# A planner that lets PV and transposes go ahead of MoE matmuls only when they can begin as early

## The chip, the cores and the metric

The kernel runs on one core of a Trainium2 chip. The metric is the time of one execution on the device, in microseconds (us). The time of a kernel is the median of three runs; beside it stands one execution taken by the hardware profiler. The core has five engines that run their own instruction queues: TensorE (PE; its weight loads are shown as PEld), VectorE (DVE), ScalarE (ACT), GpSimd (POOL) and SyncE (SP). Here POOL and SP issue the DMAs.

## What is computed

Sliding-window attention with a distance bias over 8 batches, 8 heads, 576 positions and 64 columns a head, followed by a dense layer pair with an activation on all 4608 tokens:

```python
scores = scale * np.matmul(q, k.transpose(0, 1, 3, 2))
mask = (rel >= 0) & (rel < 128)                       # rel = query position - key position
scores = np.where(mask, scores + bias[None], -1000000000.0)
attn = np.exp(scores - np.max(scores, axis=-1, keepdims=True))
attn = attn / (np.sum(attn, axis=-1, keepdims=True) + 1e-09)
x = np.matmul(attn, v)                                # then (4608, 512): heads side by side
h = x @ w_in                                          # 512 -> 2048
g = h * np.cos(h)
out = g @ w_out                                       # 2048 -> 512
```

## The kernel before

**Attention.** The work is cut into 64 units: for each batch, five blocks of 128 queries (the last of 64), the three middle blocks in two halves of four heads. Units go in pairs. For a unit TensorE makes the scores (`scores`, L556), ScalarE takes the exponential (`exps`, L583), VectorE multiplies by a table of the bias and the window (`mask`, L602), and TensorE multiplies by V with a column of ones that gives the sums (`pv`; L618 and L622 for edge blocks, L630 and L632 for middle blocks; 16 matmuls of 65 columns for a unit pair's middle blocks). VectorE divides (`norm`, L667 and L669). The result must be transposed to serve as the moving operand of the first product: on TensorE (`x_pe`, L709 and L690, and a copy to SBUF) for units that are needed soon, by a transposing DMA on SP's queue (`x_dma`) for the others.

**MoE.** Tokens go in nine chunks of 512. The first product of a chunk (`moe1`, L747; chunk 0 in smaller blocks, `moe1_block`, L772) takes 64 matmuls of 512 columns into 16 banks' worth of results; each bank gets a sine with a shifted phase on ScalarE (L752) and a multiplication on VectorE (L756) that writes `gT`. The second product (`moe2`, L800) is 64 matmuls a chunk, 16 for each 128 tokens; a copy (L807 on ScalarE or L808 on VectorE) and a store on SP follow.

**Order in the program.** For chunk c the program names the first product, then some eight units of attention that later chunks need (`QUOTA`), then the second product. The PSUM tensor `ps` has 8 banks: 0 and 1 for the second product, 2 and 3 for PV, 4 to 7 for scores; the first product of a chunk uses 2 to 7. So the first product of the next chunk comes after this chunk's attention in these banks, while the second product, in its own, can be put anywhere between.

**The planner.** The order of the instructions on each engine is not the program's: `Plan.schedule` lists the operations by a simulated clock. Each operation has an occupancy (`occ`) and a latency (`lat`) in ns, a priority (`pri`: 0 transposes, 1 PV, 2 scores, 5 first product, 6 second product) and, on TensorE, a mode (0 for MoE, PV and most transposes, 1 for scores, 2 for the transposes of q and k of the first two batches). `reach` says when an operation's inputs are there: 53 ns after the end of what another engine made, where TensorE waits. A candidate's start `st` is the later of that and of the time the engine is free; on TensorE 110 ns (`SWITCH`) are added for a change of mode, and 40 ns if the inputs come after the engine is free. `pick_pe` chooses among the candidates: `soon` is the earliest start of all; an operation with a priority under 5 that can start within an allowance of `soon` goes first, by priority; otherwise the candidate with the best priority among those that start at `soon`. Since TensorE works through its queue in the listed order, an operation that is chosen before its inputs are there holds up what is behind it.

The end of a DMA is reckoned by one of several formulas, by engine and kind; in this kernel operations with a DMA are given to "sp" and "pool" only.

Of the kernel before, what the change touches and what calls it, by code (L numbers as in the profile page):

```python
# [34 lines left out]
class Plan:  # L35
# [58 lines left out]
    def schedule(self, filler=None, fill=(0, 0)):  # L94
# [4 lines left out]
        mode, table = 0, 0  # L99
# [4 lines left out]
        def reach(o, e):  # L104
            t = 0
            for d, data in o.preds.items():
                if data == ORDER or self.held(d, data, e):
                    t = max(t, d.start + d.occ)
                elif d.dma is None and d.eng[0] == e:
                    t = max(t, d.end + 28)  # L110
                else:
                    t = max(t, d.end + (53 if e == "pe" else 36))
            return t

        def pick_pe(cand):
            soon = min(st for st, _ in cand)
            first = [(st, o) for st, o in cand if o.pri < 5 and st <= soon + 160]
            if first:
                return min(first, key=lambda c: (c[1].pri, c[1].seq))
            near = [(st, o) for st, o in cand if st <= soon]  # L120
            return min(near, key=lambda c: (c[1].pri, c[1].seq))
# [5 lines left out]
        while avail:  # L127
            phase = next((t for t in tables if left[t]), None)
            best = None
            for e in ENG:  # L130
                cand = []
                for o in avail:
                    if e not in o.eng or (o.table is not None and o.table != phase):
                        continue
                    at = reach(o, e)
                    st = max(free[e], at)
                    if e == "pe":
                        if o.mode != mode:
                            st += self.SWITCH
                        if at > free[e]:  # L140
                            st += 40
                    cand.append((st, o))
                if not cand:
                    continue
                if e == "pe":
                    st, o = pick_pe(cand)
                else:
                    soon = min(st for st, _ in cand)
                    st, o = min(((st, o) for st, o in cand if st <= soon + 40),
                                key=lambda c: (c[1].pri, c[1].seq))  # L150
                key = (st, o.pri, o.seq)
                if best is None or key < best[0]:
                    best = (key, e, o)
            (st, _, _), e, o = best
            avail.remove(o)
            if o.table is not None and o.table != table:
                st += self.TABLE
            if len(o.eng) > 1:
                o.fn, o.occ, o.lat = o.fn[e], o.occ[e], o.lat[e]
                o.eng = (e,)  # L160
            if e == "pe":
                while filler and mode == 0 and free[e] + self.FILL + 30 < st and (
                        fill[0] <= free[e] < fill[1]):
                    p = self.op("pe", filler, r=["zeros"], occ=self.FILL, lat=self.FILL + 100)
                    self.all.pop()
                    p.start, p.end = free[e], free[e] + self.FILL
                    free[e] += self.FILL
                    order.append(p)
                if st < self.COLD:
                    o.lat += o.occ  # L170
                    o.occ *= 2
            o.start = st
            free[e] = st + o.occ
            if o.dma is not None:
                if e == "sp" and o.dma[0] in "tx":
                    cross = max(cross, st + self.CROSS, min(wire + self.BACK, st + 6000)) + o.lat
                    o.end = max(cross, st + o.occ + 1400) + 500
                elif e == "sp" and o.dma[0] == "s":
                    o.end = st + o.occ + 1800 + o.lat
                elif e == "sp":  # L180
                    first = max(first, st + 1400) + o.lat
                    wire = max(wire, min(first, 5600))
                    o.end = max(first, st + o.occ + 1400) + 500
                else:
                    wire = max(wire, st + 2300) + o.lat
                    o.end = max(wire, st + o.occ + 1400) + 500
            else:
                o.end = st + o.lat
            if e == "pe":
                mode = o.mode  # L190
            if o.table is not None:
                table = o.table
                left[o.table] -= 1
            order.append(o)
            for s in o.succs:
                s.npred -= 1
                if s.npred == 0:
                    avail.append(s)
# [752 lines left out]
```

## Time and profile before

| | before |
|---|---|
| median of 3 runs | 314.29 us (313.84 to 314.87) |
| profiled execution | 314.18 us |
| its span | 312.4 us |
| TensorE matmul busy | 303.3 us, 2678 instructions |
| VectorE, ScalarE, POOL busy | 192.3, 202.4, 97.6 us |
| second product L800, first product L747 | 131.6 and 111.6 us busy |
| scores L556 | 20.7 us busy |
| PV L618, L622, L630, L632 | 8.2, 4.9, 15.0, 15.0 us busy |

Busy times of TensorE overlap where matmuls are in flight together. A row of the groups names the line, the engine, the operation, output and inputs, the shape, the count, then busy us and mean ns of one, then the engine's idle time just ahead of them and what ended most of it. A row of the timeline gives the start, the duration, the instruction, a count and, in brackets, the idle time before it. A row of the waits gives who waited for whom, then total us, number of times, and the longest. A few per cent of the matmul records are missing from the trace; the weight loads of L747 and L800 are complete (512 and 592).

### The profile page before, as it was taken

What the parts mean: (1) busy time and instruction counts of PE and PEld (TensorE: products, weight loads), DVE (VectorE), ACT (ScalarE), POOL (GpSimd) and SP (SyncE); (2) the same over time, 40 slices, a digit from 0 to 9 for tenths busy, and PEclk for the clock granted to TensorE, in tenths of its full rate; (3) what the DMA queues carried; (4) which work ended last, traced back from release to release, by engine and by line L of the source; (5) the groups of instructions that cost most, each with busy time, mean ns of one, the idle gap of its engine ahead of it and who ended that gap; (6) DMA issues with size and microseconds to landing.
All of it is one profiled execution on the core that took longest, in us unless ns stands there. A gap on an engine that the chain in (4) does not pass through costs nothing.

```text
span 312.4 us, 6647 instructions
## 1 busy us (share of the span) xinstructions
PE 303.3 (97%) x2678; PEld 160.5 (51%) x2721; DVE 192.3 (62%) x405; ACT 202.4 (65%) x270; POOL 97.6 (31%) x123
## 2 busy tenths in 40 slices
PE   7899999999999999999999999999999999999996
PEld 4689755445544454445444544455445544444444
DVE  6588667584848576748586758576766886353000
ACT  5697865885767677777677558754874868362211
POOL 8998340049132731382054605280000000000000
PEclk9999999999999999999999999999999999999999
DMA  8999999999979995999599999999641320001112
GB/s 108 163 203 207 207 168 192 177 130 179 150 118 179 96 181 111 176 110 154 94 118 149 160 117 138 155 151 131 128 109 44 78 67 2 34 0 68 69 67 101
DMA packets 150334, 38.97 MB, mean 125 GB/s; under 512 B 138912, under 2 KB 145312, under 8 KB 150304
## 3 DMA queue, kind: packets, MB, share of 16 engines
q0 software_dynamic: 100960, 18.23, 76.2%
q1 hardware_dynamic: 49344, 20.33, 31.3%
q8 instruction: 21, 0.34, 0.5%
q14 instruction: 9, 0.07, 0.1%
HBM read 36.70 MB, written 9.44 MB: 148 GB/s over the span
## 4 chain that ended last, share of the span: by engine, by line
PE 90%; DMA 3%; POOL 3%; issue 1%; DVE 1%; ACT 1%; POOLq 0%; ACTq 0%
PE ps L800 39%; PE ps L747 34%; PE ps L556 5%; PE ps L772 5%; DMA w_inb<-in_moe_w_in_dram 3%; PE ps L630 2%; PE ps L632 2%; PE ps L618 2%; POOL vp L384 1%; PE ps L497 1%; DVE gT L756 1%; POOL krows L376 1%; PE ps L622 1%; PE ps L709 1%; POOL qrows L376 0%
## 5 line engine op out<-in xcount | busy, mean ns | idle before, releaser
L800 PE MATMUL ps<-w_outb,gT 128*128 128x512 bf16 (+2 forms) x561 | 131.6, 373 | 2.3 <-issue 1.3
L747 PE MATMUL ps<-xT,w_inb 128*128 128x512 bf16 x502 | 111.6, 379 | 0.5
L756 DVE TENSOR_TENSOR gT<-ps,cos 128x512 bf16<-128x512 f32 x128 | 85.7, 689 | 40.5 <-ACT cos L752 29.8
L752 ACT ACTIVATE cos<-ps,halfpi 128x512 f32<-128x512 f32 x128 | 85.2, 687 | 22.1 <-PE ps L747 16.6
L583 ACT ACTIVATE p<-ps 128x1024 bf16<-128x1024 f32 x64 | 62.1, 1021 | 33.3 <-PE ps L556 33.2
L800 PEld LDWEIGHTS ps<-w_outb,gT 128*128 128x128 bf16 x592 | 52.8, 98 | 55.3 <-DMA w_outb<-in_moe_w_out_dram 0.2
L747 PEld LDWEIGHTS ps<-xT,w_inb 128*128 128x128 bf16 x512 | 49.8, 98 | 60.1 <-issue 0.8
L394 POOL DMA_DIRECT2D qnat<-in_q_dram x30 | 25.3, 877 | 71.3 <-DMA qt<-qnat 71.3
L602 DVE TENSOR_TENSOR p<-p,emask 128x1024 bf16<-128x1024 bf16 x59 | 39.6, 682 | 9.5 <-ACT p L583 9.3
L807 ACT ACTIVATE ob<-ps 128x512 f32<-128x512 f32 (+2 forms) x23 | 13.3, 579 | 41.7 <-PE ps L800 41.5
L384 POOL DMA_DIRECT2D vp<-in_v_dram x40 | 34.0, 896 | 9.1 <-PE ps L622 5.0
L394 POOL DMA_DIRECT2D knat<-in_k_dram x30 | 25.3, 880 | 30.7 <-DMA kt<-knat 28.3
L556 PE MATMUL ps<-qt,kt 64*128 64x128 bf16 (+1 forms) x576 | 20.7, 213 | 0.3 <-DVE qt L513 0.3
L556 PEld LDWEIGHTS ps<-qt,kt 64*128 64x128 bf16 x576 | 14.7, 95 | 11.1 <-ACT p L583 6.3
L669 DVE TENSOR_TENSOR xnat<-ps,rec 128x256 bf16<-128x256 f32 x48 | 18.3, 420 | 0.4
L808 DVE COPY ob<-ps 128x512 f32<-128x512 f32 x14 | 9.6, 687 | 13.5 <-PE ps L800 13.5
L630 PEld LDWEIGHTS ps<-vp,p 128*128 128x128 bf16 x192 | 12.7, 97 | 8.5 <-issue 8.4
L772 PE MATMUL ps<-xT,w_inb 128*128 128x128 bf16 x256 | 16.4, 219 | 0.4 <-DMA w_inb<-in_moe_w_in_dram 0.4
L630 PE MATMUL ps<-vp,p 128*128 128x65 bf16 x192 | 15.0, 193 | 0.3
L772 PEld LDWEIGHTS ps<-xT,w_inb 128*128 128x128 bf16 x256 | 14.5, 98 | 1.1 <-DMA w_inb<-in_moe_w_in_dram 0.5
L632 PE MATMUL ps<-vp,p 128*128 128x65 bf16 x192 | 15.0, 193 | 0.0
L782 DVE TENSOR_TENSOR gT<-ps,cos 128x512 bf16<-128x512 f32 x16 | 10.7, 689 | 3.2 <-ACT cos L779 2.9
(63 smaller groups left out, 159.4 us busy)
## 6 DMA issues: line engine op xcount, KB each, us to landing
out_dram<-ob SPq DMA_DIRECT2D x35, 256.0 KB, 3.6
vp<-in_v_dram POOLq DMA_DIRECT2D x32, 128.0 KB, 6.4
qnat<-in_q_dram POOLq DMA_DIRECT2D x24, 128.0 KB, 5.9
knat<-in_k_dram POOLq DMA_DIRECT2D x24, 128.0 KB, 4.8
w_outb<-in_moe_w_out_dram POOLq DMA_DIRECT2D x4, 512.0 KB, 21.7
w_inb<-in_moe_w_in_dram POOLq DMA_DIRECT2D x3, 512.0 KB, 12.1
qrows<-in_q_dram POOLq DMA_DIRECT2D x1, 576.0 KB, 15.4
krows<-in_k_dram POOLq DMA_DIRECT2D x1, 576.0 KB, 17.4
```

The lines of the kernel that those rows point to most:

```text
L384: op("pool", [lambda e, t=t, rows=rows: e.dma_start(vp[b % 2][0:rows, t, :, 0:64], v[b, :, 128 * t:128 * t + rows, :].rearrange("h p d -> ...
L394: fns.append(lambda e, t=t, rows=rows: e.dma_start(nat[which][0:rows, t, :, :], src[b, :, 128 * t:128 * t + rows, :].rearrange("h p d -> p ...
L556: ins = e.matmul(ps[:, banks[x], c0:c0 + n_], keys_ap(b, x, pr, kc), query_ap(b, x, pr, qb, n_), start=not acc, stop=stop)
L583: op("act", lambda e: e.activation(P[i][:, 0:1024], ps[:, banks[0]:banks[0] + 2, :].rearrange("p a b -> p (a b)"), ACTF.Exp, scale=0.125), ...
L602: op("dve", lambda e: e.tensor_tensor(p, p, m, ALU.mult), r=[("P", i), ("EM", 0), ("EM", 1)], w=[("P", i)], occ=600, lat=690, pri=1)
L630: e.matmul(o, P[i][:, c0:c0 + 128], V[:, qb - 1, h, 0:65], start=True, stop=False)
L632: ins = e.matmul(o, P[i][:, c0 + 128:c0 + 256], V[:, qb, h, 0:65], start=False, stop=True)
L747: op("pe", lambda e, kc=kc: e.matmul(ps[:, bank, :], w_in[:, kc, 128 * fc:128 * fc + 128], xT[:, kc, r0:r0 + CH], start=(kc == 0), stop=(k ...
L752: op("act", lambda e: e.activation(cosb[ci][:, :], ps[:, bank, :], ACTF.Sin, bias=halfpi[:, 0:1]), r=["halfpi"], w=[("B", bank), ("cos", c ...
L756: op("dve", lambda e: e.tensor_tensor(gT[gi][:, fc, :], ps[:, bank, :], cosb[ci][:, :], ALU.mult), r=[("cos", ci)], w=[("B", bank)] + [("g ...
L772: ins = e.matmul(ps[:, bank, 128 * i:128 * i + 128], w_in[:, kc, 128 * fc:128 * fc + 128], xT[:, kc, t0:t0 + 128], start=(kc == 0), stop=( ...
L800: op("pe", lambda e, t=t, fc=fc, bank=bank, j0=j0, j1=j1: e.matmul(ps[:, bank, 0:j1 - j0], gT[gi][:, fc, 128 * t:128 * t + 128], w_out[:, ...
```

## The change

Two edits in `schedule`. In `pick_pe` the allowance of 160 ns is kept for operations whose mode differs from that of TensorE's last operation; for those of the same mode it is 0. So after a MoE matmul, a PV or a transpose (mode 0), another PV or transpose is preferred over a MoE matmul only if it can start at `soon`; scores (mode 1) are still preferred up to 160 ns after it. In the reckoning of DMA ends, the branch for plain loads on "sp" now also holds for "act".

```diff
             soon = min(st for st, _ in cand)
-            first = [(st, o) for st, o in cand if o.pri < 5 and st <= soon + 160]
+            first = [(st, o) for st, o in cand if o.pri < 5 and
+                     st <= soon + (160 if o.mode != mode else 0)]
             if first:
                 return min(first, key=lambda c: (c[1].pri, c[1].seq))
...
                 elif e == "sp" and o.dma[0] == "s":
                     o.end = st + o.occ + 1800 + o.lat
-                elif e == "sp":
+                elif e == "sp" or e == "act":
                     first = max(first, st + 1400) + o.lat
```

## The prediction

> **What bounds the kernel now.** I read the page first, then the groups of instructions by line, then the waits of the weight-load unit, and then the timeline around single PV steps.
>
> ```profile
> span 312.4 us, 6647 instructions
> ...
> PE 303.3 (97%) x2678; PEld 160.5 (51%) x2721; DVE 192.3 (62%) x405; ACT 202.4 (65%) x270; POOL 97.6 (31%) x123
> ...
> PEclk9999999999999999999999999999999999999999
> ```
>
> TensorE is busy for 97% of the span, at full clock in every slice. So the time is TensorE's work plus what it loses between its instructions. Busy time alone cannot show that loss, because one matmul's tail lies over the next one's start. The groups with shapes apart give the MoE product's duration, the groups of TensorE the idle time ahead of PV, the timeline the pace:
>
> ```profile
> L800 PE MATMUL ps<-w_outb,gT 128*128 128x512 bf16 x529 | 128.1, 379 | 2.3 <-issue 1.3
> ```
>
> ```profile
> L630 PE MATMUL ps<-vp,p 128*128 128x65 bf16 x192 | 15.0, 193 | 0.3
> L618 PE MATMUL ps<-vp,p 128*128 128x65 bf16 x128 | 8.2, 193 | 0.7 <-ACT p L583 0.5
> ```
>
> ```profile
> 102.80 1.89 PE L800 MATMUL ps<-w_outb,gT 128*128 128x512 bf16 x8
> ```
>
> One MoE matmul is shown as 379 ns, but eight in a row take 1.89 us: (1890 - 379) / 7 = 216 ns from start to start. A matmul that starts up to 379 - 216 = 163 ns late therefore leaves no idle time in the matmul rows, and PV's idle of 0.3 and 0.7 us is only the rest. I count lost time from start to start, over 216 ns. The weight loads show it more openly:
>
> ```profile
> PEld ps L630 <- issue: 8.4, 22, 0.5
> ...
> PEld ps L618 <- issue: 3.7, 11, 0.6
> ...
> PEld ps L709 <- DVE xnat L669: 1.8, 7, 0.4
> ```
>
> These are the first loads of PV (L630 for the middle blocks, L618 for the edge blocks) and of the transposes of normalised tiles (L709). Part of each wait is harmless. Compare a PV that was late with one that was not:
>
> ```profile
> 182.27 0.69 DVE L602 TENSOR_TENSOR p<-p,emask 128x1024 bf16<-128x1024 bf16 x1
> 182.70 0.38 PE L800 MATMUL ps<-w_outb,gT 128*128 128x512 bf16 x1
> 183.07 0.10 PEld L630 LDWEIGHTS ps<-vp,p 128*128 128x128 bf16 x1 [0.48 <-issue]
> 183.10 0.19 PE L630 MATMUL ps<-vp,p 128*128 128x65 bf16 x1
> ```
>
> ```profile
> 41.88 0.59 PE L800 MATMUL ps<-w_outb,gT 128*128 128x512 bf16 x2
> 42.10 0.10 PEld L618 LDWEIGHTS ps<-vp,p 128*128 128x128 bf16 x1
> 42.31 0.19 PE L618 MATMUL ps<-vp,p 128*128 128x65 bf16 x1
> ```
>
> In the second, the load is made 0.21 us ahead, under the MoE matmul before it, and PV follows without a loss. In the first, the multiplication by the mask ends at 182.27 + 0.69 = 182.96, PV starts 0.14 us after that, and it is 183.10 - 182.70 = 0.40 us behind the MoE matmul: 0.40 - 0.216 = 0.18 us are lost. Its load had idled 0.48 us, so an idle time up to 0.48 - 0.18 = 0.30 us costs nothing, and all above it is TensorE time lost. MoE matmuls that were ready stood behind PV in the queue for that long.
>
> **The change part by part.**
>
> The second edit (what a DMA from ACT is reckoned at) costs nothing: every operation with a DMA in this kernel is given to SP or to POOL, so the added case never occurs.
>
> The first edit acts where TensorE's last operation has mode 0 (MoE, PV, transposes) and a PV or a transpose could begin up to 160 ns after the MoE matmul that could begin at once. The old rule took PV there; the new one takes the MoE matmul and looks again 216 ns later. No instruction is added or removed. Which PVs are these? The planner adds 40 ns when data come late, so the allowance covers data up to 120 ns late. It counts 53 ns from VectorE's end to TensorE's start, where the rows above show 140: about 90 more. So a PV that the old rule took early should lose between 0.09 and 0.21 us on the chip, and one that the planner held ready less than 0.09. In idle time of its load that is 0.39 to 0.51 against under 0.39. Thirteen of the PV loads behind a MoE matmul have 0.43 to 0.51, and none has more. The first, the largest and the last of the thirteen:
>
> ```profile
> 47.27 0.10 PEld L630 LDWEIGHTS ps<-vp,p 128*128 128x128 bf16 x1 [0.43 <-issue]
> ...
> 242.83 0.10 PEld L630 LDWEIGHTS ps<-vp,p 128*128 128x128 bf16 x1 [0.51 <-issue]
> ...
> 248.74 0.10 PEld L630 LDWEIGHTS ps<-vp,p 128*128 128x128 bf16 x1 [0.43 <-issue]
> ```
>
> That the largest stops where the allowance ends is why I take these waits for the planner's choice. The thirteen idle 6.1 us in all; less 13 x 0.30 = 3.9 this is 2.2 us lost, about 0.17 each. Behind one more MoE matmul such a PV has its data 216 - 120 = 96 ns ahead or more by the planner's clock. The chip needs 90 of these, so the whole wait goes, not only the planned part: **-2.2 us**.
>
> The Trainium skill, TensorE: Matmul & The Clock Gate, section Back-to-back issue gap, gives about 131 ns per matmul of 512 columns as the sustained rate. By that one MoE matmul would not cover waits above 131 ns, and an estimated 0.5 us of the 2.2 would stay. The trace disagrees, with its 216 ns.
>
> The transposes have the same edit but less to give, because the chip starts them sooner than the planner thinks:
>
> ```profile
> 116.90 0.81 PE L800 MATMUL ps<-w_outb,gT 128*128 128x512 bf16 x3
> ...
> 117.58 0.11 PEld L709 LDWEIGHTS ps<-ident,xnat 128*128 128x128 bf16 x2 [0.36 <-DVE xnat L669]
> 117.58 0.28 PE L709 MATMUL ps<-ident,xnat 128*128 128x128 bf16 x2
> ```
>
> The last of the three MoE matmuls starts at 116.90 + 0.81 - 0.38 = 117.33, so the transpose loses 117.58 - 117.33 - 0.216 = 0.03 us. Three of the seven waits are of this kind: **-0.1 us**.
>
> What comes back: deferred steps shift TensorE's grid, and other PVs meet it at new places. A PV held ready by less than 90 ns still stalls. If PVs fall evenly over the 216 ns between two starts, 90/216 of them wait, 45 ns on the mean, 19 over all; for the 22 + 11 = 33 waits of L630 and L618 that is 0.6 us, against about 0.3 that the waits shorter than the thirteen hold now. **+0.3 us**; the bounds are -0.3 (all go) and 33 x 45 ns - 0.3 = +1.2 (each meets the mean).
>
> The deferred PV itself delays what waits for it, by 216 - 170 = some 50 ns on the mean: the normalisation on VectorE, the transposes (over SP's queue for most units), the banks for the next pair's PV, POOL's loads of V into the buffer that a batch has left, and the next chunk's first product. The cover is the second product (L800), which TensorE has in reserve. Up to the starts of chunks 1, 2, 3 and 4 so many of its loads were made (the second x):
>
> ```profile
> 0.00:55.10 55.10, 14.12 (x55) 5.08 (x60) 1.00 1.47 178
> 0.00:88.70 88.70, 29.66 (x118) 11.10 (x128) 1.00 1.56 172
> 0.00:120.20 120.20, 42.80 (x170) 15.89 (x184) 1.00 1.54 162
> 0.00:151.90 151.90, 56.48 (x226) 20.96 (x242) 1.00 1.50 157
> ```
>
> Of 64 a chunk, 4, 0, 8 and 14 were left. The tight one is the second:
>
> ```profile
> 87.23 1.42 PEld L800 LDWEIGHTS ps<-w_outb,gT 128*128 128x128 bf16 x8
> 88.77 0.31 PEld L747 LDWEIGHTS ps<-xT,w_inb 128*128 128x128 bf16 x2
> ```
>
> ```profile
> 87.68 0.76 DVE L669 TENSOR_TENSOR xnat<-ps,rec 128x256 bf16<-128x256 f32 x2
> ```
>
> Eight matmuls of 216 ns follow the last PV of that chunk; the normalisation that frees its banks ends at 87.68 + 0.76 = 88.44, 0.33 us before the next chunk's load. So one matmul may be taken from behind this PV at no cost, a second for 0.1: **+0.1**, between 0 and 0.2.
>
> Where PV and scores are both near, scores keep the allowance and can now go first:
>
> ```profile
> 109.10 0.19 PE L622 MATMUL ps<-vp,p 128*128 128x65 bf16 x1
> 109.23 0.62 PE L556 MATMUL ps<-qt,kt 64*128 64x128 bf16 x16
> ```
>
> Scores start 0.13 us behind PV's last matmul, where PV's own matmuls follow each other at 30 ns: 0.10 for the change of mode. Swapping the two does not change the number of such changes: 0. A pair that is torn apart would pay 0.1, and I take the same for the way back.
>
> In the first 20 us there is little MoE work to put in front, and steps of attention may change places among themselves. The trace shows no such order. TensorE has 20 - 16.57 = 3.4 us idle there, and one step moved is a scores group, 0.6 us by the row above:
>
> ```profile
> 0.00:20.00 20.00, 16.57 (x244) 11.72 (x247) 12.97 (x48) 14.18 (x18) 18.86 (x30) 1.00 1.23 151
> ```
>
> I take 0, since with that much idle time TensorE mostly waits for loads there, and keep -0.5 and +0.6 for the range.
>
> Sum: -2.2 - 0.1 + 0.3 + 0.1 = -1.9 us. The profiled execution took 314.18 us (1.8 around its span), so 312.3; the median of the runs is 314.29, 0.1 above it, so **312.4 us**. Ends: -2.2 - 0.1 - 0.3 - 0.5 = -3.1 gives 311.2, and -2.3 + 1.2 + 0.2 + 0.6 = -0.3 gives 314.0.
>
> **The rivals.** A measurement of this kernel can tell about 0.3%, 0.94 us, from no change.
>
> Only what the matmul rows show as idle can be won: 0.3 + 0.7 = 1.0 us, 313.3. For it: the rest lies under a running matmul's tail. Against: 216 ns from start to start holds wherever nothing waits, so a late start moves all that follows. The Trainium skill, Perfetto Trace Analysis, calls matmul busy time a bad metric at its opening, because matmuls are pipelined. Chance 0.08, 0.05 of it beyond 0.94 us.
>
> Nothing moves: the planner held these PVs ready, the masks came late on the chip, and the new rule picks as the old one did. 314.3. For it: the planner's times are reckoned, and the chip's may lag by as much. Against: a lag has no reason to stop at 0.51, where the allowance ends. Chance 0.09.
>
> Slower: the reserve of the second product runs out in chunks 0 to 2 before the next chunk's first matmul may start. From PV's last load (just ahead of 87.23) to the banks' release pass 88.44 - 87.23 = 1.2 us, all of it idle if no reserve is left by then: 3 x 1.2 = 3.6, less the 1.9 won, +1.7 and 316.0. It decides once more matmuls are drawn ahead than the 4, 1 and 8 that are to spare, by some 13 more over the three (2.8 us, the 1.9 and the 0.94). For it: chunk 1 ends at exactly 128, and every wait removed draws a matmul ahead. Against: of the thirteen only 1, 1 and 3 lie in these chunks. Chance 0.11.
>
> **How the numbers follow.** The forecast has 0.68. That the first 20 us alone decide has 0.04, half of it faster and a quarter each for the others. Faster by over 0.3%: 0.68 + 0.05 + 0.02 = 0.75. Within 0.3%: 0.03 + 0.09 + 0.01 = 0.13. Slower: 0.11 + 0.01 = 0.12. The range is 311.2 to 314.8: the forecast's own ends are 311.2 and 314.0, and 314.8 takes in the rival in which nothing moves with half of the 0.94 above it; the slower one is left out.
>
> **What would show it.** Right: at most four PV loads behind a MoE matmul idle over 0.40 us; the waits of L630 and L618 fall together from 12.1 us towards 10; the instruction counts stay; the gain grows by some 0.1 to 0.5 us a chunk up to 251 us, and stays to the end. Wrong: the same thirteen idle times (nothing moved); new waits of L747 for VectorE at the starts of chunks 1 to 3 (the reserve is gone); or waits of 0.31 to 0.39 at most PVs (the 90 ns came back).

## The result and the profile after

| | before | changed |
|---|---|---|
| median (22 runs each) | 314.92 us (313.84 to 316.75) | 313.44 us (312.26 to 316.94) |
| ratio | | 0.9958, 95% interval 0.9939 to 0.9977 |
| profiled execution, span | 314.18, 312.4 us | 314.44, 312.5 us |

The change makes the kernel faster by 0.42%, 1.3 us (0.7 to 1.9). The profiled execution of the changed kernel is one of its longer ones: its span shows no gain at all. That is the first thing to read from its page, where DMAs and SP's queue stand in the chain that ended last, which they did not to this extent before:

```profile
span 312.5 us, 6695 instructions
...
PE 304.3 (97%) x2722; PEld 160.9 (51%) x2722; DVE 191.2 (61%) x401; ACT 204.9 (66%) x274; POOL 97.6 (31%) x123
...
PE 83%; DMA 7%; SPq 4%; POOL 3%; ACT 1%; issue 1%; DVE 0%; POOLq 0%; ACTq 0%
```

The waits of the weight loads (who waited for whom, total us, times, longest) have the gain and what took it back:

```profile
PEld ps L631 <- issue: 6.0, 20, 0.5
...
PEld ps L619 <- issue: 2.8, 10, 0.5
...
PEld ps L748 <- issue: 1.9, 3, 1.4
PEld ps L557 <- DMA kt<-knat: 1.6, 2, 1.2
...
PEld ps L619 <- DMA vp<-in_v_dram: 0.7, 1, 0.7
PEld ps L631 <- DMA vp<-in_v_dram: 0.7, 2, 0.4
...
PEld ps L748 <- DVE xnat L670: 0.4, 2, 0.2
```

(All lines are one higher than before.) PV's own waits went from 8.4 + 3.7 to 6.0 + 2.8 and the 1.4 that are put down to V, and the transposes' row is gone. Two long waits are new: 1.37 us of the first product (L748) at the start of chunk 6 and 1.16 us of the scores (L557) in chunk 5. On the timeline:

```profile
200.98 0.14 PEld L557 LDWEIGHTS ps<-qt,kt 64*128 64x128 bf16 x6 [1.16 <-DMA kt<-knat]
...
217.94 0.13 PEld L748 LDWEIGHTS ps<-xT,w_inb 128*128 128x128 bf16 x2 [1.37 <-issue]
217.97 0.38 PE L748 MATMUL ps<-xT,w_inb 128*128 128x512 bf16 x1 [0.90 <-DMA xT<-xfirst]
```

The second product still had matmuls to give at that place (369 of 384 loads made), but they are listed behind the first product's. From start to start the wait of the scores cost 0.83 us and that of the first product 1.07: 1.9 us in this execution.

The PV of 108.65, which before was 0.20 us late, shows the change itself. Before:

```profile
105.43 3.19 PE L800 MATMUL ps<-w_outb,gT 128*128 128x512 bf16 x14 [0.16 <-issue]
108.62 0.10 PEld L618 LDWEIGHTS ps<-vp,p 128*128 128x128 bf16 x1 [0.50 <-issue]
```

It now stands behind one more MoE matmul. The last of the three starts at 107.89 + 0.81 - 0.38 = 108.32, and PV follows at 0.22 us, its load idle for a harmless 0.28:

```profile
107.89 0.81 PE L801 MATMUL ps<-w_outb,gT 128*128 128x512 bf16 x3
...
108.48 0.10 PEld L619 LDWEIGHTS ps<-vp,p 128*128 128x128 bf16 x1 [0.28 <-issue]
108.54 0.19 PE L619 MATMUL ps<-vp,p 128*128 128x65 bf16 x1
```

A kernel's time has three parts that the profiles keep apart: the first 36 us, the stretch from the first to the last load of the second product, and a tail of 2.7 us. The middle one, called the stretch below, is read from one row of a kernel, the first and last start of the loads. Before and changed:

```profile
L800 PEld LDWEIGHTS ps<-w_outb,gT x592: 95/98/99, 35.7 to 309.7; 128*128 128x128 bf16 x198
```

```profile
L801 PEld LDWEIGHTS ps<-w_outb,gT x592: 95/98/99, 36.1 to 309.8; 128*128 128x128 bf16 x198
```

That is 274.0 and 273.7 us: 0.3 less, with 1.9 us of late DMAs in it.

### The profile page after: what moved, and what is told of

Same layout as the page of the kernel before. It is cut to its first block, busy times and chain, and to the rows that moved or that the text cites. A ratio compares the mean times of both kernels' runs of the same rounds, so it can differ in the third digit from the quotient of the medians.

```text
span 312.5 us, 6695 instructions
## 1 busy us (share of the span) xinstructions
PE 304.3 (97%) x2722; PEld 160.9 (51%) x2722; DVE 191.2 (61%) x401; ACT 204.9 (66%) x274; POOL 97.6 (31%) x123
## 4 chain that ended last, share of the span: by engine, by line
PE 83%; DMA 7%; SPq 4%; POOL 3%; ACT 1%; issue 1%; DVE 0%; POOLq 0%; ACTq 0%
PE ps L801 37%; PE ps L748 31%; PE ps L557 5%; PE ps L773 4%; DMA w_inb<-in_moe_w_in_dram 3%; DMA xT<-xfirst 3%; SPq L404 2%; DMA kt<-knat 2%; SPq L735 2%; PE ps L631 1%; PE ps L633 1%; PE ps L619 1%; POOL vp L385 1%; PE ps L498 1%; POOL krows L377 1%
## 5 line engine op out<-in xcount | busy, mean ns | idle before, releaser
L801 PE MATMUL ps<-w_outb,gT 128*128 128x512 bf16 (+2 forms) x592 | 136.5, 374 | 0.0
L748 PE MATMUL ps<-xT,w_inb 128*128 128x512 bf16 x512 | 112.3, 379 | 0.9 <-DMA xT<-xfirst 0.9
L757 DVE TENSOR_TENSOR gT<-ps,cos 128x512 bf16<-128x512 f32 x128 | 86.1, 689 | 41.3 <-ACT cos L753 30.3
L748 PEld LDWEIGHTS ps<-xT,w_inb 128*128 128x128 bf16 x512 | 49.8, 98 | 61.2 <-issue 1.9
L808 ACT ACTIVATE ob<-ps 128x512 f32<-128x512 f32 (+2 forms) x25 | 14.5, 581 | 41.3 <-PE ps L801 41.2
L557 PE MATMUL ps<-qt,kt 64*128 64x128 bf16 (+1 forms) x576 | 20.5, 211 | 1.2 <-DMA kt<-knat 0.7
L557 PEld LDWEIGHTS ps<-qt,kt 64*128 64x128 bf16 x576 | 14.6, 94 | 11.7 <-ACT p L584 5.9
L631 PEld LDWEIGHTS ps<-vp,p 128*128 128x128 bf16 x192 | 12.9, 97 | 6.8 <-issue 6.0
L631 PE MATMUL ps<-vp,p 128*128 128x65 bf16 x192 | 15.1, 193 | 0.4 <-DMA vp<-in_v_dram 0.2
L809 DVE COPY ob<-ps 128x512 f32<-128x512 f32 x12 | 8.2, 680 | 9.8 <-PE ps L801 9.8
L633 PEld LDWEIGHTS ps<-vp,p 128*128 128x128 bf16 x192 | 12.5, 97 | 0.1
```

The source lines that it names most:

```text
L557: ins = e.matmul(ps[:, banks[x], c0:c0 + n_], keys_ap(b, x, pr, kc), query_ap(b, x, pr, qb, n_), start=not acc, stop=stop)
L631: e.matmul(o, P[i][:, c0:c0 + 128], V[:, qb - 1, h, 0:65], start=True, stop=False)
L633: ins = e.matmul(o, P[i][:, c0 + 128:c0 + 256], V[:, qb, h, 0:65], start=False, stop=True)
L748: op("pe", lambda e, kc=kc: e.matmul(ps[:, bank, :], w_in[:, kc, 128 * fc:128 * fc + 128], xT[:, kc, r0:r0 + CH], start=(kc == 0), stop=(k ...
L757: op("dve", lambda e: e.tensor_tensor(gT[gi][:, fc, :], ps[:, bank, :], cosb[ci][:, :], ALU.mult), r=[("cos", ci)], w=[("B", bank)] + [("g ...
L801: op("pe", lambda e, t=t, fc=fc, bank=bank, j0=j0, j1=j1: e.matmul(ps[:, bank, 0:j1 - j0], gT[gi][:, fc, 128 * t:128 * t + 128], w_out[:, ...
```

## The experiments

The theory to start with (A): the change wins 2 us of PV stalls, and the late DMAs are its own doing. In chunks 4 and 5 the new plan puts the transposing DMAs of q ahead of two x transposes on SP's queue (180.91 in place of 184.49, 213.71 in place of 216.84), where they run beside POOL's loads of V. The rival (B): such waits come and go from run to run.

**SP's order undone, and SP's order alone.** In the changed kernel the q transposes of chunks 4 and 5 are put back; in the kernel before they are brought forward. All other queues keep their order.

```diff
+        sp = [o for o in self.order if o.eng[0] == "sp"]
+        for q in [o for o in sp if o.dma in ("trq0", "trq1")][4:6]:
+            i = sp.index(q)
+            q.start = [o for o in sp[i:] if o.dma[0] == "x"][1].start + 1      # undone
+            # alone: [o for o in sp[:i] if o.dma[0] == "x"][-2].start - 1
+        self.order.sort(key=lambda o: (o.start, rank[id(o)]))
```

> The changed kernel with one thing undone: in chunks 4 and 5 the transposing DMAs of q go back behind the two x transposes that stood ahead of them before the change; every other queue keeps the order of the changed kernel. Theory A (the change won about 2 us of PV stalls, and part of it was given back because it pulled the q transposes ahead of two x transposes on SP's queue, so that they run into POOL's loads of V): the 1.07 us wait of the first product at the start of chunk 6 and the 0.83 us wait of the scores in chunk 5 shrink below 0.3 us each, the x transposes of chunk 5 land within 0.5 us of 216.5, and the ratio to the kernel before is 0.990 to 0.994 (311.8 to 313.0 us). Rival B (such waits for DMAs come and go from run to run, whatever the order): waits of 0.5 us or more appear here as well, and the ratio stays at 0.996.

> The kernel before with one thing of the change alone: in chunks 4 and 5 the transposing DMAs of q are put ahead of the two x transposes, as the change did; TensorE's order is that of before. Theory A (the order on SP's queue costs): the last x transposes of chunk 5 that chunk 6 needs land at 217.5 to 218.5 in place of 216.8, TensorE waits there, and the time is 0.5 to 1.5 us over the kernel before (ratio 1.002 to 1.005). Rival B (run to run): same time, ratio 0.998 to 1.002, the waits of PV unchanged.

Undone: 314.23 us, ratio 0.9984 (0.9965 to 1.0003), no better than the change as it is; by the times alone no gain over the kernel before is clear here. Alone: 314.44 us, ratio 1.0003 (0.9984 to 1.0023). Late DMAs appear in both, at other places: at the start of chunk 5 in the first, and of chunk 3 in the second, whose SP queue is that of the kernel before up to there.

```profile
185.48 0.11 PEld L753 LDWEIGHTS ps<-xT,w_inb 128*128 128x128 bf16 x2 [0.87 <-DMA xT<-xnat]
```

```profile
122.84 0.11 PEld L752 LDWEIGHTS ps<-xT,w_inb 128*128 128x128 bf16 x2 [1.32 <-DMA xT<-xnat]
```

So the part of theory A on SP's order falls: undoing it wins nothing, and the wait turns up with TensorE's old order too.

**The rule for PV alone.**

```diff
-                     st <= soon + (160 if o.mode != mode else 0)]
+                     st <= soon + (0 if o.mode == mode and o.pri == 1 else 160)]
```

> The new rule for PV alone; transposes and the first matmuls with the bias keep the allowance of 160 ns. Theory A (the gain is in PV; the transposes lose only 0.03 us each, and the first 40 us are 0.3 us later in the changed kernel because steps of the start changed places there): stalls of PV as in the changed kernel (0.6 us in all after 20 us), the first load of the second product at 35.7 us as before and not at 36.1, SP's order as in the changed kernel, so ratio 0.993 to 0.997. Rival C (the transposes carry the gain, or the whole start is needed): ratio 0.998 to 1.000.

313.25 us, ratio 0.996 (0.9942 to 0.9978), the same as the whole change. The gain is PV's. The first load of the second product came at 37.0 us here and not at the 35.7 expected, though TensorE's order at the start is that of before: the first 36 us vary from run to run by more than the 0.3 us that I had wanted to explain.

**A larger allowance.** 320 ns in place of 0.

> The allowance for operations of the same mode is 320 ns in place of 0 (160 before). Theory A (a PV taken before its data holds up ready MoE matmuls, and all that time is lost to TensorE): nearly every PV and transpose is taken early, some 45 of them by 55 to 340 ns by the planner's clock, 10.7 us in all, and the chip adds up to 90 ns to each PV; so 9 to 14 us over the kernel before, 324 to 329 us. Rival D (TensorE's rest hides under matmul tails or is made up later, because something else paces the chunks): under 4 us slower, 319 us at most.

324.70 us, ratio 1.0313 (1.028 to 1.0345): 9.8 us slower, in the range of theory A. The waits of the same three rows grow to

```profile
PEld ps L631 <- issue: 10.6, 21, 0.7
PEld ps L619 <- issue: 6.3, 13, 1.0
...
PEld ps L710 <- DVE xnat L670: 4.4, 12, 0.6
```

from 8.4, 3.7 and 1.8, by 7.4 us in all, and the stretch grows by 8.9:

```profile
L801 PEld LDWEIGHTS ps<-w_outb,gT x592: 95/98/99, 38.1 to 321.0; 128*128 128x128 bf16 x198
```

So nothing later made the waits up. They are not all of the 9.8 us: this execution also has two late DMAs (0.80 us of the scores at 167.83, 1.17 of the first product at 184.94) and a later first load, and these were not taken apart.

**POOL's loads cut**, in the order of before, of the change, and of the next experiment. Later batches of V, q and k load 8 rows of each tile only, and the rest of the work runs on old rows.

```diff
-                    vp[b % 2][0:rows, t, :, 0:64],
-                    v[b, :, 128 * t:128 * t + rows, :].rearrange("h p d -> p h d"))],
+                    vp[b % 2][0:real, t, :, 0:64],                 # real: 8 from batch 2 on
+                    v[b, :, 128 * t:128 * t + real, :].rearrange("h p d -> p h d"))],
...
-                rows = 128 if t < 4 else 64
+                rows = (128 if t < 4 else 64) if b < 3 else 8
```

> The kernel before with POOL's traffic cut: of V from batch 2 on and of q and k from batch 3 on only 8 rows of each tile are loaded (the rest of the computation runs on old rows); the order on every engine is that of before. Theory A (PV and transposes lose about 2.5 us between the planner's choice and the semaphore; the late DMAs at chunk starts are loads in the way and cost the kernel before something too): no wait of the first product or of the scores for a DMA after 40 us, stalls of PV as before (about 2.9 us), 0 to 1 us under the kernel before: ratio 0.997 to 1.000. Rival B (these DMAs are late by themselves): waits for a DMA of 0.5 us or more after 40 us stay, ratio 0.999 to 1.001.

> The changed kernel with the same traffic cut; the order on every engine is that of the changed kernel. Theory A (the change wins 2.0 us of stalls on TensorE, and late DMAs take back 0.7 us of it on the mean because a faster TensorE meets them more often): 1.8 to 2.3 us under the run of the kernel before with the same cut, ratio to the kernel before 0.990 to 0.993. Rival E (late DMAs strike both orders alike, and the change is worth only the 1.3 us that the times show, the first 40 us giving back the rest): 1.0 to 1.5 us under it, and the first 40 us are longer by 0.3 us or more.

Before with the cut: 314.47 us, ratio 0.9995 (0.9976 to 1.0015). Changed with the cut: 313.18 us, ratio 0.993 (0.9902 to 0.9957). The two ratios lie 0.65% apart, 2.0 us, where they lie 0.42% apart with all loads; their intervals are too wide to call the difference shown, and the medians lie only 1.3 us apart, which is rival E's range. The six runs of the changed kernel lie in two groups, four near 313.2 and two near 311.9. No wait of the first product or of the scores for a DMA of 0.3 us or more is left after 40 us in either profile. Cutting the traffic does not make the kernel before faster: it has little to lose to late DMAs, by the interval under 0.8 us. The stretch is 273.9 us before and 272.0 changed, so the 2.0 us of theory A are won there; whether the start gives some back, as E has it, one profile each (first load at 36.4 and 36.6) cannot tell:

```profile
L801 PEld LDWEIGHTS ps<-w_outb,gT x592: 95/98/99, 36.4 to 310.3; 128*128 128x128 bf16 x198
```

```profile
L802 PEld LDWEIGHTS ps<-w_outb,gT x592: 95/98/99, 36.6 to 308.6; 128*128 128x128 bf16 x198
```

**The planner told what the chip takes.** The changed kernel, with 146 ns from another engine's end to a PV.

```diff
-                    t = max(t, d.end + (53 if e == "pe" else 36))
+                    t = max(t, d.end + (36 if e != "pe" else 146 if o.pri == 1 else 53))
```

> The changed kernel, with the planner told 146 ns in place of 53 from another engine's end to a PV. Theory A (what is left of PV's stalls, 0.6 us, is the difference between the 53 that the planner reckons and what the chip takes): PV stalls of over 50 ns after 20 us vanish but for two at most, 0.3 to 0.7 us under the changed kernel, ratio to the kernel before 0.993 to 0.995. Rival F (what is left are masks that come late on the chip for other reasons, or late DMAs hide the difference): three or more stalls over 100 ns stay, or the ratio is 0.995 to 0.998.

> The kernel with the planner told 146 ns, with the same traffic cut as the two quiet runs. Theory A: 0.3 to 0.7 us under the changed kernel with the cut. Rival F: within 0.2 us of it.

312.30 us, ratio 0.9914 (0.9888 to 0.994), the fastest version here: faster than the kernel before, and 1.1 us under the changed kernel by the medians, though the intervals of the two ratios just meet. Of the PV loads behind a MoE matmul none idles over 0.40 us, where before had thirteen and the change two. Past 20 us, and beyond the harmless 0.30 each (0.304 before rounding), they idle 2.46 us in all before, 0.60 after the change and 0.18 here. With POOL's loads cut it takes 312.37 us (0.9916, 0.989 to 0.9941), 0.8 us under the changed kernel with the cut, with intervals that overlap. Both differences are above the 0.3 to 0.7 us expected. The stretch is 307.7 - 36.2 = 271.5 us, 0.5 under the changed kernel's 272.0, which is in theory A's range:

```profile
PEld ps L631 <- issue: 4.9, 17, 0.3
PEld ps L619 <- issue: 2.7, 10, 0.5
```

```profile
L801 PEld LDWEIGHTS ps<-w_outb,gT x592: 95/98/99, 36.2 to 307.7; 128*128 128x128 bf16 x198
```

**Both kernels again**, two more profiles each, to see where late DMAs fall.

> The changed kernel again, for a second profile. Theory G (its order makes late DMAs its own: the first product waits at the starts of chunk 5 or 6 in every execution): 0.5 us or more of waits of the first product or the scores for a DMA after 180 us. Theory B (late DMAs fall at random, in either kernel): none, or elsewhere; the PV stalls are the same 0.6 us in both cases.

> The changed kernel a third time. Theory G: 0.5 us or more of such waits after 180 us. Theory B: none, or elsewhere.

> The kernel before again. Theory G: no wait for a DMA of over 0.3 us after 40 us. Theory B: such a wait is as likely here as in the changed kernel; the PV stalls are the same 2.9 us in both cases.

> The kernel before a third time. Theory G: no wait for a DMA of over 0.3 us after 40 us. Theory B: as likely here as in the changed kernel.

The changed kernel took 311.98 and 313.05 us, the kernel before 315.35 and 314.22. No first product or scores wait 0.5 us for a DMA in any of the four past 40 us. So theory G, that the new order makes them in every execution, falls. First and last load of the second product, changed and then before:

```profile
L801 PEld LDWEIGHTS ps<-w_outb,gT x592: 95/98/99, 35.4 to 307.4; 128*128 128x128 bf16 x198
```

```profile
L801 PEld LDWEIGHTS ps<-w_outb,gT x592: 95/98/99, 36.4 to 308.4; 128*128 128x128 bf16 x198
```

```profile
L800 PEld LDWEIGHTS ps<-w_outb,gT x592: 95/98/99, 36.9 to 310.8; 128*128 128x128 bf16 x198
```

```profile
L800 PEld LDWEIGHTS ps<-w_outb,gT x592: 95/98/99, 35.7 to 309.7; 128*128 128x128 bf16 x198
```

| from first to last load of the second product | us |
|---|---|
| TensorE's order of before | 274.0, 273.9, 274.0; loads cut 273.9; q early 275.0 |
| changed | 273.7, 272.0, 272.0; loads cut 272.0; q late 272.5; PV alone 272.1 |
| told 146 ns | 271.5; loads cut 271.6 |

Without a late DMA an order gives the same stretch to 0.1 us every time. The three that stand out (273.7, 272.5, 275.0) are those with late DMAs, and each is longer by about what TensorE waited for them (1.9, 0.5 and 1.0 us from start to start).

## Why the prediction was right, and where it was off

The forecast was 1.9 us below the kernel before, 312.4 us from the 314.29 of three runs. The runs that followed put the kernel before at 314.92, and the 313.44 of the changed kernel is 1.3 us below it by the ratio: the sign and the mechanism hold, the size is two thirds.

**The stalls: right.** The sum had -2.2 for the thirteen PVs, -0.1 for the transposes and +0.3 for what comes back, -2.0 together. The undisturbed stretches give 274.0 - 272.0 = 2.0 us. In all thirteen the load starts 0.12 us behind a VectorE end, the mask's in eight and in five that of the division (L658) that frees PV's banks. The transposes are worth about the 0.1 they were given: with the rule for PV alone the stretch is 272.1. The waits of L631 and L619 fall to 9.6 and 9.7 us in the two profiles without late DMAs, towards 10 as forecast. What comes back was sized at 0.6 us of remaining stalls, from a uniform spread over 216 ns; the loads show 0.60. That these agree so closely is luck: 0.3 of the 0.60 are two waits of 0.46 and 0.48 us, longer than the 0.39 that the sizing allowed.

**"I take these waits for the planner's choice": right for nine of the thirteen.** The plan itself tells. In the starts that `schedule` of the kernel before computes, ten PVs past 20 us are chosen before their inputs are there, by 62 to 120 ns: nine of the thirteen and the PV of 52.94, whose load idled 0.39. The other four (140.12, 183.07, 215.90 and 248.74) start in the plan when TensorE is free, with their inputs there; on the chip each load starts 0.12 us behind the end of its mask, so the mask came later than planned. They hold 0.6 of the 2.2 us, and 183.07 is the PV that the prediction took as its example. So a PV that the planner held ready could lose 0.13 to 0.18 us, not less than 0.09, and the argument that 0.51 is the allowance's end could not tell the two kinds apart. That three of these four lost most of their wait all the same, as the PVs ahead of them moved, is luck. The fourth, the last PV of chunk 5, stands where it stood, behind the same number of second products; before and changed:

```profile
215.90 0.10 PEld L630 LDWEIGHTS ps<-vp,p 128*128 128x128 bf16 x1 [0.48 <-issue]
```

```profile
214.73 0.59 PE L801 MATMUL ps<-w_outb,gT 128*128 128x512 bf16 x2
215.31 0.10 PEld L631 LDWEIGHTS ps<-vp,p 128*128 128x128 bf16 x1 [0.48 <-issue]
```

It went down to 0.34 only when the planner reckoned with 146 ns. A latency reckoned too short thus made part of the stalls that I had put down to the allowance. That this one remained and another came up in chunk 4 (171.97, 0.46 idle) is within what was allowed for ("at most four").

**The reserve, the scores, the start: 0.1, 0 and 0.** No new wait of the first product for VectorE came up (the row of L748 for VectorE's xnat above: 0.4 us in two waits, as before), so the +0.1 was not paid. Scores did not overtake PV: past 10 us the steps of attention follow each other on TensorE in the same order in both kernels. For the first 36 us the profiles cannot decide: with the start of before the first load of the second product came between 35.7 and 37.0, with the new one between 35.4 and 36.6. Neither order is seen to be ahead.

**What the sum left out:** late DMAs. I looked for them only as a reserve that runs dry and as 50 ns on SP's queue. Where one comes, it costs 0.5 to 1.1 us, half of the gain, and TensorE's list then holds ready matmuls back in the same way as an early PV did. The times show 1.3 us (0.7 to 1.9) where the stalls are worth 2.0. Late DMAs of this size struck two of the five profiles with the new rule, all loads and 53 ns, and one of the four with the old order. These are few, and the spans of all executions say more. An estimate: the mean span less the order's undisturbed stretch and the tail is what the start and late DMAs take together.

| mean span less stretch and tail | us |
|---|---|
| TensorE's order of before (29 and 17 runs; loads cut 12; q early 12) | 36.1 and 36.3; 36.1; 36.2 |
| changed (22 runs; loads cut 6; q late 12; PV alone 12) | 37.1; 36.1; 37.5; 36.7 |
| told 146 ns (6 runs; loads cut 6) | 36.1; 36.0 |

The standard errors are 0.1 to 0.3 us. So with all loads and 53 ns the new rule does lose some 0.5 to 1.4 us more there than the old one, which is not seen with the loads cut and there speaks against rival E. That is the size of the missing 0.7, and another 0.1 lies outside the span (1.92 us of an execution of the changed kernel, 1.80 of the kernel before). Why the planner told 146 ns is spared, and how the loss is shared between the start and late DMAs, stays open; SP's order is not the cause, since with q late the loss is no smaller.

The other rivals: the idle time of the matmul rows (1.0 us) was no bound, since 2.0 us came off. "Nothing moves" and the reserve that runs out are refuted by the waits.

By the 131 ns for a matmul of the Trainium skill (TensorE: Matmul & The Clock Gate, section Back-to-back issue gap) an estimated 0.5 us of waits would have stayed at the thirteen places. The trace after the change has the same 216 ns from start to start, and PVs moved by one matmul, as at 108.54, have no wait left.

## What to carry to other kernels

Where one engine is the bound and works through a list, an operation that is listed before its inputs are there costs all of its wait that the work ahead does not cover, and nothing downstream gave it back here; allow for it only where no ready work could go first. Read such waits from start to start, or at the weight loads, since the matmul rows hid most of them. Which waits a rule has chosen is read from the plan, not from their size: four of the thirteen were not the allowance's. A planner's latencies should be measured at the very edge that it orders by: 53 ns reckoned for 146 cost the stretch another 0.5 us beside the 2.0 that the change won.

## What the runs showed of the hardware

An execution's first 36 us vary by 1.6 us (first load of the second product at 35.4 to 37.0) and a DMA that is late at a chunk's start by up to 1.1 us more, while the 272 us between repeat to 0.1 us where no DMA is late. One profile of such a kernel can show a change of 0.5% with the wrong sign, as the first pair here did.
